# Another set of hand-set ranks for a scan-and-adapters kernel, with some gate steps and copies on other engines

## The chip, the core and the metric

The kernel runs on one core of a Trainium2 chip. The metric is the device time of one execution in microseconds (us); of several runs the median is given. A profiled execution has a time of its own and a span, which reaches from its first to its last instruction. A core has five engines that run side by side, each with its own queue of instructions, worked off in order: TensorE (PE in the profile; its weight loads are listed as PEld), VectorE (DVE), ScalarE (ACT), GpSimd (POOL) and SyncE (SP), which here only issues DMA transfers. PSUM is the memory that PE writes to, in eight banks; SBUF is the larger on-chip memory.

## The reference, cut to what matters

```python
def _attn_ref(a, b):              # a, b: (8, 6400, 128)
    for t in range(S):
        h = a[:, t] * h + b[:, t]
        out[:, t] = h
def _moe_ref(x, w_gate, A, B):    # x: out as (51200, 128); E = 8 adapters of rank 16
    logits = x @ w_gate
    topk = np.argpartition(-logits, 2, axis=1)[:, :2]
    w = exp(sel - max); w /= w.sum() + 1e-9
    delta[mask] += w[mask, k] * ((x[mask] @ A[e]) @ B[e])
    return x + delta
```

A linear recurrence along each of 8 sequences gives x. Then every one of the 51,200 rows goes through the two of eight small adapters whose logits are highest, weighted by a softmax over those two, and x is added. Read and written are 52.6 and 26.2 MB.

## The kernel before, in words

The rows are cut into 100 chunks of 512 rows (4 blocks of 128). A chunk goes through two halves.

The **front** of chunk c: a load of a and one of b bring two chunks (512 KB each) into one of 6 slots (line 709); PE transposes a into a bank of pA and b into a bank of pB (line 730; operations A, B and P); ScalarE copies pA to a_st (line 748, ae); VectorE runs the recurrence over 512 columns with one scan instruction (line 786, sc), which writes xT. Each scan needs the one before it.

Six blocks make a **unit**: PE multiplies xT with the adapters' A and the gate weights side by side (line 806, Z) and ScalarE copies the result to zl (line 812, ze). Four units make a **group** of 24 blocks; the first groups and the last ones are smaller, and the last four (18 to 21) hold a single chunk each. For a group the **gate** is worked out in small steps, named by kind and group, as 3_2 for kind 3 of group 2: kind 1, the largest logit (line 861, or 857 in groups of one chunk); 2, the difference to it (843 or 868); 3 and 5, the largest one masked out (845, 848); 4, the second largest (850); 6, the difference to that (852 or 870); 7, the sum of both (874); w1, a sigmoid on ScalarE (876); 8, the weights g (882). Kinds 1, 4 and 8 always run on VectorE. Kinds 2, 3, 5, 6 and 7 run on GpSimd, unless the list GATE_DVE names them.

The **back** of a chunk: zw = zl times g (line 915 on GpSimd, mu; line 919 on VectorE for the chunks in MU_DVE, md); PE transposes zw into a bank (928, T); a copy brings it to zwT (te: line 934 on ScalarE for the chunks in TE_ACT, else line 937 on VectorE); PE adds xT and zwT times B up in the same bank (942 and 943, D); a copy brings the result to outt (line 957 on ScalarE, oe; line 954 on VectorE for the chunks in OE_DVE, od); a store takes two chunks to the output, of the last four chunks one (line 988, st). outt holds 18 chunks. The banks of pO are used in turn for the back; for the last 12 chunks those of pA and pB are used too.

**What sets the order.** Nothing of this order is written in the program's text as such. Every operation has a rank, a base that grows with its chunk, plus an entry of TEMPLATE by its kind and its place in a period of six chunks, plus an entry of NUDGE by its name. `Program.schedule` (line 332) goes through a model of the engines with operations sorted by rank on each: an engine takes the one of lowest rank once its inputs are there by the model, and if no engine can go on, the operation that could start first of all. The result is one fixed list for each engine, and `waits` (line 402) puts in the semaphore waits. A rank is thus a wish; where an operation's inputs come later than its rank, others go ahead only when all engines are stuck. SyncE's list holds loads (la, lb) and stores (st) in one queue, and a load waits there until PE has read the slot's earlier content.

Of the kernel before, what the change touches and what calls it, by code (L numbers as in the profile page):

```python
# [30 lines left out]
    "A0": 332.698, "A1": 444.438, "A2": 395.795, "A3": 404.345, "A4": 42.259, "B0": 448.161, "B1": 453.245, "B2":  # L31
    404.853, "B3": 403.799, "B99": 126.44, "D0": 64.669, "D1": 46.767, "D10": 83.067, "D11": 50.451, "D12": 30.005,
    "D13": 96.239, "D14": 46.691, "D15": 42.568, "D16": 45.565, "D17": 47.157, "D18": 49.305, "D19": 50.496, "D2":
    38.555, "D20": 51.923, "D21": 47.721, "D22": 49.736, "D23": 51.873, "D24": 54.021, "D25": 55.177, "D26": 56.604,
    "D27": 52.402, "D28": 54.23, "D29": 56.021, "D3": 33.278, "D30": 58.169, "D31": 59.312, "D32": 60.739, "D33":
    56.537, "D34": 58.365, "D35": 60.156, "D36": 62.304, "D37": 63.447, "D38": 64.874, "D39": 60.672, "D4": 32.746,
    "D40": 62.5, "D41": 64.291, "D42": 67.109, "D43": 67.982, "D44": 69.439, "D45": 65.237, "D46": 67.065, "D47":
    68.968, "D48": 71.116, "D49": 72.307, "D5": 37.683, "D50": 73.734, "D51": 69.532, "D52": 71.36, "D53": 73.151,
    "D54": 75.554, "D55": 76.442, "D56": 77.884, "D57": 73.682, "D58": 75.51, "D59": 78.992, "D6": 33.975, "D60":
    80.547, "D61": 81.42, "D62": 82.877, "D63": 79.28, "D64": 79.738, "D65": 84.028, "D66": 84.486, "D67": 87.103,  # L40
    "D68": 88.306, "D69": 84.321, "D7": 39.991, "D70": 86.2, "D71": 87.403, "D72": 90.164, "D73": 91.555, "D74":
    93.991, "D75": 88.603, "D76": 92.856, "D77": 92.398, "D78": 96.983, "D79": 95.164, "D8": 78.702, "D80": 99.794,
    "D81": 93.491, "D82": 115.278, "D83": 119.134, "D84": 158.466, "D85": 222.925, "D86": 154.578, "D87": 119.577,
    "D88": 117.659, "D89": 187.618, "D9": 48.932, "D90": 118.7, "D91": 181.167, "D92": 131.702, "D93": 144.905,
    "D94": 212.656, "D95": 160.549, "D96": 168.236, "D97": 95.555, "D98": 78.117, "D99": 130.788, "P10": 15.657,
    "P11": 22.702, "P12": 39.886, "P13": 53.646, "P14": 28.955, "P15": 9.673, "P16": 15.966, "P17": 18.415, "P18":
    15.425, "P19": 16.467, "P20": 18.575, "P21": 20.345, "P22": 21.434, "P23": 23.734, "P24": 20.558, "P25": 21.527,
    "P26": 22.774, "P27": 25.117, "P28": 26.674, "P29": 27.984, "P30": 24.567, "P31": 25.76, "P32": 28.665, "P33":
    31.023, "P34": 32.839, "P35": 33.584, "P36": 30.178, "P37": 31.969, "P38": 33.403, "P39": 35.194, "P4": 49.375,
    "P40": 37.555, "P41": 38.3, "P42": 34.859, "P43": 36.65, "P44": 38.084, "P45": 39.912, "P46": 41.703, "P47":  # L50
    42.448, "P48": 38.994, "P49": 40.785, "P5": 25.498, "P50": 42.219, "P51": 44.047, "P52": 45.838, "P53": 46.583,
    "P54": 43.129, "P55": 44.92, "P56": 46.354, "P57": 48.182, "P58": 49.973, "P59": 51.388, "P6": 21.844, "P60":
    47.694, "P61": 49.485, "P62": 50.919, "P63": 52.747, "P64": 54.65, "P65": 55.395, "P66": 51.989, "P67": 53.78,
    "P68": 55.214, "P69": 57.042, "P7": 43.001, "P70": 58.833, "P71": 59.833, "P72": 56.139, "P73": 57.93, "P74":
    59.364, "P75": 61.192, "P76": 62.525, "P77": 64.45, "P78": 61.014, "P79": 62.469, "P8": 16.186, "P80": 65.142,
    "P81": 67.722, "P82": 69.826, "P83": 70.391, "P84": 67.243, "P85": 68.614, "P86": 69.735, "P87": 76.775, "P88":
    74.219, "P89": 78.609, "P9": 48.708, "P90": 71.884, "P91": 73.91, "P92": 151.293, "P93": 167.423, "P94": 136.89,
    "P95": 80.922, "P96": 88.01, "P97": 133.589, "P98": 99.826, "T0": 56.382, "T1": 91.427, "T10": 73.644, "T11":
    39.89, "T12": 41.046, "T13": 32.168, "T14": 85.598, "T15": 40.536, "T16": 43.441, "T17": 44.977, "T18": 47.615,
    "T19": 49.081, "T2": 99.35, "T20": 50.954, "T21": 46.745, "T22": 48.179, "T23": 49.148, "T24": 52.331, "T25":  # L60
    53.797, "T26": 55.635, "T27": 51.426, "T28": 52.86, "T29": 54.688, "T3": 26.004, "T30": 56.479, "T31": 57.945,
    "T32": 59.77, "T33": 55.561, "T34": 56.995, "T35": 58.823, "T36": 60.614, "T37": 62.08, "T38": 63.905, "T39":
    59.696, "T4": 30.392, "T40": 61.13, "T41": 62.958, "T42": 64.749, "T43": 66.885, "T44": 68.47, "T45": 64.261,
    "T46": 65.695, "T47": 67.523, "T48": 69.426, "T49": 70.892, "T5": 35.969, "T50": 72.765, "T51": 68.556, "T52":
    69.99, "T53": 71.818, "T54": 73.609, "T55": 75.33, "T56": 76.915, "T57": 72.706, "T58": 74.14, "T59": 75.968,
    "T6": 44.458, "T60": 77.301, "T61": 80.323, "T62": 81.908, "T63": 77.335, "T64": 78.671, "T65": 81.565, "T66":
    82.439, "T67": 85.689, "T68": 86.658, "T69": 82.764, "T7": 38.572, "T70": 84.097, "T71": 85.976, "T72": 87.861,
    "T73": 89.94, "T74": 92.377, "T75": 87.346, "T76": 89.832, "T77": 90.32, "T78": 95.622, "T79": 94.176, "T8":
    37.375, "T80": 98.697, "T81": 90.642, "T82": 104.934, "T83": 107.397, "T84": 147.188, "T85": 128.013, "T86":
    190.078, "T87": 133.961, "T88": 186.597, "T89": 94.992, "T9": 42.025, "T90": 132.176, "T91": 95.557, "T92":  # L70
    169.538, "T93": 158.037, "T94": 309.895, "T95": 232.152, "T96": 128.695, "T97": 143.342, "T98": 164.952, "T99":
    82.392, "Z0": -4.337, "Z1": 19.058, "Z10": 20.035, "Z11": 18.061, "Z12": 19.964, "Z13": 22.981, "Z14": 26.095,
    "Z15": 23.194, "Z16": 25.272, "Z17": 27.295, "Z18": 29.086, "Z19": 26.745, "Z2": 33.243, "Z20": 29.505, "Z21":
    33.201, "Z22": 34.768, "Z23": 32.132, "Z24": 34.381, "Z25": 37.372, "Z26": 39.509, "Z27": 36.813, "Z28": 39.062,
    "Z29": 41.866, "Z3": 20.134, "Z30": 43.657, "Z31": 40.948, "Z32": 43.197, "Z33": 46.001, "Z34": 47.792, "Z35":
    45.083, "Z36": 47.332, "Z37": 50.136, "Z38": 51.927, "Z39": 49.567, "Z4": 8.718, "Z40": 51.897, "Z41": 54.701,
    "Z42": 56.492, "Z43": 53.943, "Z44": 56.192, "Z45": 58.996, "Z46": 60.787, "Z47": 58.078, "Z48": 60.342, "Z49":
    63.146, "Z5": 29.08, "Z50": 64.937, "Z51": 63.005, "Z52": 65.559, "Z53": 69.201, "Z54": 71.664, "Z55": 70.67,
    "Z56": 72.956, "Z57": 75.978, "Z58": 78.531, "Z59": 74.133, "Z6": 18.876, "Z60": 75.768, "Z61": 79.931, "Z62":
    81.463, "Z63": 79.056, "Z64": 80.664, "Z65": 116.582, "Z66": 110.873, "Z67": 170.833, "Z68": 78.231, "Z7":  # L80
    52.026, "Z8": 23.141, "Z9": 12.774, "ae0": 377.319, "ae1": 447.239, "ae10": 20.203, "ae11": 45.845, "ae12":
    26.555, "ae13": 114.601, "ae14": 78.247, "ae15": -8.915, "ae16": 9.547, "ae17": 35.333, "ae18": 14.62, "ae19":
    16.327, "ae2": 430.204, "ae20": 17.024, "ae21": 19.433, "ae22": 21.246, "ae23": 22.239, "ae24": 18.539, "ae25":
    21.584, "ae26": 22.556, "ae27": 23.782, "ae28": 26.079, "ae29": 27.602, "ae3": 401.457, "ae30": 23.062, "ae31":
    25.957, "ae32": 28.958, "ae33": 29.47, "ae34": 31.955, "ae35": 33.668, "ae36": 29.441, "ae37": 31.155, "ae38":
    32.869, "ae39": 34.329, "ae4": 24.476, "ae40": 36.772, "ae41": 38.486, "ae42": 34.157, "ae43": 35.871, "ae44":
    37.584, "ae45": 38.889, "ae46": 40.717, "ae47": 42.508, "ae48": 38.305, "ae49": 40.019, "ae5": 44.251, "ae50":
    41.733, "ae51": 43.092, "ae52": 44.852, "ae53": 46.643, "ae54": 42.44, "ae55": 44.154, "ae56": 45.868, "ae57":
    47.159, "ae58": 48.987, "ae59": 50.778, "ae6": 13.042, "ae60": 47.245, "ae61": 48.959, "ae62": 50.673, "ae63":
    51.895, "ae64": 53.609, "ae65": 55.455, "ae66": 51.252, "ae67": 52.966, "ae68": 54.68, "ae69": 56.087, "ae7":  # L90
    61.054, "ae70": 57.847, "ae71": 59.638, "ae72": 55.69, "ae73": 57.404, "ae74": 59.117, "ae75": 60.339, "ae76":
    62.053, "ae77": 65.098, "ae78": 61.47, "ae79": 61.896, "ae8": 2.461, "ae80": 63.047, "ae81": 66.773, "ae82":
    69.416, "ae83": 71.087, "ae84": 65.544, "ae85": 67.471, "ae86": 72.468, "ae87": 71.251, "ae88": 123.456, "ae89":
    94.229, "ae9": 43.382, "ae90": 106.289, "ae91": 132.603, "ae92": 144.806, "ae93": 134.759, "ae94": 74.716,
    "ae95": 79.344, "ae96": 74.12, "ae97": 78.144, "ae98": 107.257, "ae99": 242.941, "cc": 482.303, "ch": 444.183,
    "cm": 407.091, "g1_0": -93.951, "g1_1": 24.384, "g1_10": 53.547, "g1_11": 58.272, "g1_12": 62.407, "g1_13":
    66.495, "g1_14": 73.075, "g1_15": 96.367, "g1_16": 144.379, "g1_17": 89.89, "g1_18": 186.375, "g1_19": 157.094,
# [1009 lines left out]
```

## Time and profile before

| what | value |
|---|---|
| median of 3 runs | 202.56 us (202.31 to 202.83) |
| profiled execution, its own time | 202.71 us |
| its span | 200.9 us |
| granted clock of TensorE, mean | 0.992 |
| moved by DMA | 79.26 MB |

How to read what follows: a row of a group has line, engine, operation, names and shapes, count, busy time and mean length of one. A row of a timeline has start, length, engine, line, operation, output and inputs, the count, and in brackets how long the engine had been idle and what ended it; rows of one kind that follow one another are merged. A row of a window has its limits and length, the busy time of the five engines' columns, the granted clock, the share of time that the 16 DMA engines were busy, and the GB/s. Tiles go by the program's names without buffer numbers.

### The profile page before, as it was taken

What the parts mean: (1) busy time and instruction counts of PE and PEld (TensorE: products, weight loads), DVE (VectorE), ACT (ScalarE), POOL (GpSimd) and SP (SyncE); (2) the same over time, 40 slices, a digit from 0 to 9 for tenths busy, and PEclk for the clock granted to TensorE, in tenths of its full rate; (3) what the DMA queues carried; (4) which work ended last, traced back from release to release, by engine and by line L of the source; (5) the groups of instructions that cost most, each with busy time, mean ns of one, the idle gap of its engine ahead of it and who ended that gap; (6) DMA issues with size and microseconds to landing.
All of it is one profiled execution on the core that took longest, in us unless ns stands there. A gap on an engine that the chain in (4) does not pass through costs nothing.

```text
span 200.9 us, 7616 instructions
## 1 busy us (share of the span) xinstructions
PE 179.4 (89%) x3192; PEld 156.7 (78%) x3192; DVE 175.8 (88%) x283; ACT 175.7 (87%) x327; POOL 136.6 (68%) x176
## 2 busy tenths in 40 slices
PE   6988888999899989996998999889999998998970
PEld 6876767888678878886887888778887887887850
DVE  1599899999999988998797999898899999999970
ACT  2479898999879989998897999899989998999870
POOL 1331549598999988697787797867956657867320
PEclk9999999999999999999999999999999999999996
DMA  6999999999999999999999999999999999999985
GB/s 211 399 410 405 407 409 402 409 409 404 420 400 402 393 415 404 408 413 411 408 412 409 410 409 416 413 409 410 412 410 409 417 411 408 402 385 385 373 339 203
DMA packets 29065, 79.26 MB, mean 395 GB/s; under 512 B 2664, under 2 KB 2920, under 8 KB 29032
## 3 DMA queue, kind: packets, MB, share of 16 engines
q1 hardware_dynamic: 28456, 78.39, 98.9%
q8 instruction: 25, 0.41, 0.8%
q10 hardware_dynamic: 576, 0.40, 0.6%
q14 instruction: 8, 0.07, 0.1%
HBM read 52.56 MB, written 26.21 MB: 392 GB/s over the span
## 4 chain that ended last, share of the span: by engine, by line
DMA 33%; PE 28%; ACT 8%; DVE 8%; issue 1%; SPq 1%; ACTq 0%
DMA a_tm<-in_a_dram 26%; DMA b_tm<-in_b_dram 7%; PE pO L942 5%; PE pZ L806 4%; PE pB L730 4%; PE pA L730 4%; DVE xT L786 4%; PE pO L928 4%; PE pO L943 4%; ACT zl L812 3%; ACT a_st L748 2%; ACT outt L957 2%; ACT zwT L934 1%; DVE zwT L937 1%; SPq L709 1%
## 5 line engine op out<-in xcount | busy, mean ns | idle before, releaser
L786 DVE TENSOR_TENSOR_SCAN xT<-a_st,xT,pB 128x512 f16<-128x512 f32 x96 | 120.5, 1255 | 6.5 <-PE pA L730 2.9
L915 POOL TENSOR_TENSOR zw<-zl,g 128x512 f16<-128x512 f32 x88 | 92.7, 1066 | 26.5 <-DVE g L882 19.3
L730 PE MATMUL pB<-ident_f,b_tm 64*128 64x64 f32 (+1 forms) x784 | 69.6, 230 | 6.1 <-DMA a_tm<-in_a_dram 5.6
L730 PE MATMUL pA<-ident_f,a_tm 64*128 64x64 f32 (+1 forms) x784 | 69.7, 230 | 0.6 <-DMA b_tm<-in_b_dram 0.3
L748 ACT COPY a_st<-pA 128x512 f32<-128x512 f32 x100 | 62.9, 634 | 4.9 <-PE pA L730 3.6
L730 PEld LDWEIGHTS pB<-ident_f,b_tm 64*128 64x128 f32 (+1 forms) x784 | 56.7, 139 | 11.1 <-DMA a_tm<-in_a_dram 7.3
L812 ACT COPY zl<-pZ 128x816 f32<-128x816 f32 (+1 forms) x69 | 59.6, 863 | 2.4 <-PE pZ L806 2.3
L730 PEld LDWEIGHTS pA<-ident_f,a_tm 64*128 64x128 f32 (+1 forms) x784 | 56.8, 139 | 6.1 <-DMA b_tm<-in_b_dram 0.7
L957 ACT COPY outt<-pO 128x512 f32<-128x512 f32 x87 | 55.0, 641 | 2.5 <-PE pO L943 2.2
L942 PE MATMUL pO<-ident_h,xT 128*128 128x128 f16 x368 | 51.4, 222 | 1.3 <-ACT zwT L934 1.1
L943 PE MATMUL pO<-cst_h,zwT 128*128 128x128 f16 x368 | 50.3, 219 | 0.0
L942 PEld LDWEIGHTS pO<-ident_h,xT 128*128 128x128 f16 x368 | 40.3, 113 | 4.4 <-ACT zwT L934 1.6
L806 PE MATMUL pZ<-cst_h,xT 128*128 128x136 f16 x400 | 36.0, 225 | 4.0 <-DVE xT L786 2.0
L943 PEld LDWEIGHTS pO<-cst_h,zwT 128*128 128x128 f16 x368 | 36.8, 100 | 0.0
L928 PE MATMUL pO<-ident_h,zw 128*128 128x128 f16 x368 | 35.2, 220 | 1.4 <-DVE outt L954 0.5
L806 PEld LDWEIGHTS pZ<-cst_h,xT 128*128 128x128 f16 x400 | 26.2, 115 | 8.6 <-DVE xT L786 4.2
L928 PEld LDWEIGHTS pO<-ident_h,zw 128*128 128x128 f16 x368 | 22.7, 97 | 4.9 <-issue 1.3
L937 DVE COPY zwT<-pO 128x512 f16<-128x512 f16 x57 | 23.0, 409 | 4.0 <-PE pO L928 3.6
L934 ACT COPY zwT<-pO 128x512 f16<-128x512 f16 x35 | 21.8, 627 | 4.4 <-PE pO L928 4.0
L852 POOL TENSOR_TENSOR L<-k,m 128x192 f32<-128x192 f32 (+2 forms) x16 | 8.3, 519 | 6.5 <-DVE m L850 6.5
L874 POOL TENSOR_TENSOR k<-k,L 128x192 f32<-128x192 f32 (+1 forms) x17 | 9.4, 554 | 4.5 <-DVE L L870 3.2
L848 POOL TENSOR_TENSOR L<-L,k 128x192 f32<-128x192 f32 (+1 forms) x15 | 8.6, 576 | 5.4 <-DVE L L845 4.7
(58 smaller groups left out, 113.3 us busy)
## 6 DMA issues: line engine op xcount, KB each, us to landing
a_tm<-in_a_dram SPq DMA_DIRECT2D x48, 512.0 KB, 13.1
b_tm<-in_b_dram SPq DMA_DIRECT2D x48, 512.0 KB, 13.2
out_dram<-outt SPq DMA_DIRECT2D x47, 512.0 KB, 13.1
a_tm<-in_a_dram SPq DMA_DIRECT2D x4, 256.0 KB, 4.2
out_dram<-outt SPq DMA_DIRECT2D x4, 256.0 KB, 4.0
b_tm<-in_b_dram SPq DMA_DIRECT2D x3, 256.0 KB, 5.7
out_dram<-outt SPq DMA_DIRECT2D x1, 496.0 KB
b_tm<-in_b_dram ACTq DMA_DIRECT2D x1, 256.0 KB, 3.4
```

Of the source, the lines that this page charges most:

```text
L730: last = eng["pe"].transpose(*args)
L748: lambda: eng["act"].copy(a_st[c % NA][:, :], pA[:, c % 2, :]), fr(c, "ae"))
L786: last = eng["dve"].tensor_tensor_scan(out=x[:, s0:s1], data0=a_st[c % NA][:, s0:s1], data1=pB[:, c % 2, s0:s1], initial=init, op0=ALU.mul ...
L806: last = eng["pe"].matmul(pZ[:, k // (n // 2), o : o + W], xblock(b0 + k), Awg_h)
L812: return eng["act"].copy(zl[:, zb : zb + n, :].rearrange("p (h k) w -> p h (k w)", h=2), pZ[:, :, 0 : n // 2 * W])
L915: lambda: eng["pool"].tensor_tensor(out=wv, in0=zv, in1=gv, op=ALU.mult), ba(gi, c, "mu"))
L928: last = eng["pe"].transpose(ptile[:, k * 128 : k * 128 + 128], zz[:, k, :], ident_h[:, :])
L934: lambda: eng["act"].copy(zt, ptile[:, 0 : n * 128]), ba(gi, c, "ta"))
L937: lambda: eng["dve"].tensor_copy(zt, ptile[:, 0 : n * 128]), ba(gi, c, "te"))
L942: eng["pe"].matmul(dst, xblock(b0 + k), ident_h[:, :], start=True, stop=False)
L943: last = eng["pe"].matmul(dst, zt[:, k * 128 : k * 128 + 128], B_h, start=False, stop=True)
L957: lambda: eng["act"].copy(ov, bv), ba(gi, c, "oe"))
```

## The change

The ranks come from another seed of the same search. The program's code is the same; only constants differ.

```diff
-GATE_DVE = ['2_0', '2_14', '2_18', '3_1', '3_11', '3_13', '3_15', '3_16', '3_2', '3_8', '5_14', '5_17', '6_0', '6_18', '6_3', '7_1', '7_17', '7_18', '7_20', '7_21']
+GATE_DVE = ['2_14', '2_18', '3_1', '3_11', '3_13', '3_15', '3_16', '3_8', '5_14', '5_17', '6_3', '7_17', '7_18', '7_2', '7_20', '7_21']
...
-TE_ACT = [0, 1, 2, 6, 7, 11, 12, 19, 22, 24, 25, 30, 31, 36, 37, 42, 43, 48, 49, 54, 55, 59, 60, 61, 67, 68, 69, 73, 75, 78, 80, 82, 83, 87, 92, 93, 95, 96, 97, 98]
+TE_ACT = [0, 1, 2, 6, 7, 11, 12, 19, 24, 25, 30, 31, 36, 37, 42, 43, 48, 49, 54, 55, 60, 61, 67, 68, 69, 73, 74, 75, 78, 80, 82, 83, 87, 90, 92, 93, 94, 95, 96, 97, 98]
 MU_DVE = [61, 72, 77, 82, 86, 91, 92, 93, 94, 96, 97, 99]
-OE_DVE = [11, 15, 72, 81, 92, 94, 97]
+OE_DVE = [11, 15, 72, 81, 86, 92, 94, 96, 97]
...
 TEMPLATE = {
-    "la": [0.617, 1.382, -0.181],
-    "lb": [0.289, -1.881, 0.376],
+    "la": [1.102, 2.627, 1.579],
+    "lb": [2.514, 4.938, 1.652],
...
-    "sc": [-0.352, 0.601, 0.068, 1.247, 29.666, -1.078],
+    "sc": [-0.772, -0.302, -0.229, 45.175, 60.592, -0.968],
...
-    "st": [2.655, 0.241, 1.338],
+    "st": [2.764, 1.849, -0.699],
```

The templates of the other kinds differ in the same way, most by less than 1 where the middle of the run uses them. Of NUDGE, some 480 of 1,288 entries differ, nearly all for chunks below 18 and from 78 on; the entries of the middle are the same, such as these:

```python
"lb56": 32.697, "la58": 33.962, "st24": 58.826, "st26": 61.432, "st28": 65.231
```

The list of gate steps on VectorE has 16 names and had 20 (2_0, 3_2, 6_0, 6_18 and 7_1 leave, 7_2 comes). ScalarE's list of zwT copies has 41 chunks and had 40 (22 and 59 leave, 74, 90 and 94 come). VectorE's list of output copies has 9 and had 7 (86 and 96 come). Number, shapes and contents of all operations and transfers are the same.

More of the change, by code (lines that the diff above doesn't have):

```diff
@@ L245 @@
 TEMPLATE = {
-    "la": [0.617, 1.382, -0.181],
-    "lb": [0.289, -1.881, 0.376],
-    "A": [0.0, 0.0, 0.0, 0.0, -22.609, 0.0],
-    "B": [0.016, -0.127, 0.808, 0.22, 0.59, 0.13],
-    "ae": [0.478, 0.108, 0.156, -0.214, 0.098, 0.802],
-    "sc": [-0.352, 0.601, 0.068, 1.247, 29.666, -1.078],
-    "Z": [0.074, 0.124, 0.07, -0.415],
-    "ze": [0.146, 0.091, -0.438, 0.663],
-    "g1": [0.736],
-    "g2": [-2.194],
-    "g3": [-0.858],
-    "g4": [-0.178],
-    "g5": [18.025],
-    "g6": [22.851],
-    "w1": [-0.215],
+    "la": [1.102, 2.627, 1.579],
+    "lb": [2.514, 4.938, 1.652],
+    "A": [0.0, 0.0, 0.0, 0.0, 8.835, 0.0],
+    "B": [0.009, -0.256, 0.344, -0.056, 1.151, 0.453],
+    "ae": [0.72, 0.104, -0.01, 0.181, 0.043, 0.887],
+    "sc": [-0.772, -0.302, -0.229, 45.175, 60.592, -0.968],
+    "Z": [-0.11, 0.237, -0.045, -0.342],
+    "ze": [0.744, -0.171, -0.004, 0.826],
+    "g1": [13.688],
+    "g2": [5.03],
+    "g3": [-2.196],
+    "g4": [-1.086],
+    "g5": [31.806],
+    "g6": [21.26],
+    "w1": [-0.301],
     "w2": [0.0],
@@ L264 @@
     "p3": [0.0],
-    "mu": [1.432, -0.247, 0.712, 0.979, 0.638, 1.684],
-    "T": [-0.04, 0.011, 0.309, 0.056, 0.263, 0.069],
-    "te": [-0.194, -0.349, -1.1, 4.512, 0.878, -1.627],
-    "D": [0.293, 0.3, -0.403, 0.26, 0.471, 0.206],
-    "oe": [-0.17, -1.066, 0.732, 0.378, -0.33, -0.315],
-    "st": [2.655, 0.241, 1.338],
-    "ta": [0.113, -0.235, -1.676, 1.106, 0.524, -0.261],
-    "md": [60.131, 24.961, 1.624, -2.633, 1.124, -17.851],
+    "mu": [-0.029, -0.944, -0.301, 0.352, 0.288, 1.547],
+    "T": [-0.048, -0.432, 0.073, 0.471, 0.308, 0.135],
+    "te": [-0.952, -0.199, -0.346, 14.078, -4.494, -2.03],
+    "D": [-0.056, 0.355, -0.103, 0.22, 0.375, 0.132],
+    "oe": [-0.295, -0.102, 0.821, 0.666, 0.029, -0.305],
+    "st": [2.764, 1.849, -0.699],
+    "ta": [30.336, -6.933, -5.212, 1.29, 0.829, 38.329],
+    "md": [43.885, 7.675, 42.269, -10.074, -0.09, -40.307],
     "wu": [0.0],
     "fi": [0.0, 0.0, 0.0, 0.0, 0.0, 0.0],
-    "ch": [53.69],
-    "cm": [11.639],
-    "cc": [8.728],
+    "ch": [92.955],
+    "cm": [20.146],
+    "cc": [40.014],
     "mb": [0.0],
-    "q2": [-0.491],
-    "q3": [-4.197],
-    "q5": [-3.568],
-    "q6": [0.447],
-    "q7": [0.367],
+    "q2": [0.997],
+    "q3": [-4.705],
+    "q5": [-3.63],
+    "q6": [-0.349],
+    "q7": [-0.116],
     "q8": [0.0],
-    "g7": [19.938],
-    "g8": [-0.285],
+    "g7": [-14.036],
+    "g8": [-0.055],
 }
```

350 rows, old and new, of the table NUDGE are left out of this document.

## The prediction

> **What bounds the kernel now.** I read first the page's top, for engine totals and the slices, and then the tables by window, from coarse to fine.
>
> ```profile
> span 200.9 us, 7616 instructions
> ## 1 busy us (share of the span) xinstructions
> PE 179.4 (89%) x3192; PEld 156.7 (78%) x3192; DVE 175.8 (88%) x283; ACT 175.7 (87%) x327; POOL 136.6 (68%) x176
> ...
> GB/s 211 399 410 405 407 409 402 409 409 404 420 400 402 393 415 404 408 413 411 408 412 409 410 409 416 413 409 410 412 410 409 417 411 408 402 385 385 373 339 203
> ...
> q1 hardware_dynamic: 28456, 78.39, 98.9%
> ```
>
> No engine is full over the whole span, but the DMA queue q1 is, at 98.9%. From the second slice to the 34th it moves about 410 GB/s. Only the last six slices (5.02 us each) fall away. The reader is to see two regimes: a long middle in which the transfers set the pace whatever the engines do, and a tail of some 30 us in which they don't.
>
> ```profile
> 140.00:160.00 20.00, 18.94 (x358) 16.63 (x357) 18.67 (x29) 19.22 (x37) 13.99 (x17) 1.00 1.03 410
> 160.00:170.00 10.00, 9.25 (x169) 7.84 (x167) 9.59 (x15) 9.03 (x18) 6.20 (x9) 1.00 1.04 413
> 170.00:175.00 5.00, 4.67 (x93) 4.09 (x91) 5.00 (x9) 5.00 (x10) 4.18 (x6) 1.00 1.01 401
> ...
> 180.00:185.00 5.00, 4.36 (x66) 3.68 (x65) 5.00 (x21) 4.92 (x11) 3.89 (x5) 1.00 1.04 395
> ```
>
> The columns are PE, PEld, VectorE, ScalarE and GpSimd busy, then the granted clock, the DMA share and GB/s. In the middle VectorE still has 1.3 us free in 20 (18.67). From 170 us it has none, and at 180 to 185 ScalarE has almost none. So in the tail VectorE is the engine to watch. In the finer windows:
>
> ```profile
> 185.00:186.00 1.00, 1.00 (x21) 0.95 (x19) 0.60 (x3) 0.67 (x2) 1.00 (x4) 1.00 0.89 340
> ...
> 188.00:189.00 1.00, 0.89 (x10) 0.51 (x10) 1.00 (x7) 1.00 (x4) 0.00 (x0) 1.00 0.87 334
> ...
> 191.00:192.00 1.00, 0.36 (x7) 0.18 (x4) 1.00 (x3) 0.83 (x2) 0.95 (x1) 1.00 0.90 336
> 192.00:193.00 1.00, 0.93 (x12) 0.69 (x12) 0.97 (x5) 0.94 (x3) 0.00 (x0) 1.00 0.52 195
> ```
>
> The DMA engines go hungry there: 0.11 + 0.13 + 0.10 + 0.48 = 0.82 us of idle transfer time in these four microseconds. Who keeps them hungry is seen in VectorE's own timeline:
>
> ```profile
> 189.36 0.41 DVE L937 COPY zwT<-pO 128x512 f16<-128x512 f16 x1
> 189.74 0.22 DVE L874 TENSOR_TENSOR k<-k,L 128x32 f32<-128x32 f32 x1
> 189.88 0.78 DVE L919 TENSOR_TENSOR zw<-zl,g 128x512 f16<-128x512 f32 x1
> 190.62 0.19 DVE L882 SCALAR_TENSOR_TENSOR g<-L,sd 128x32 f32<-128x32 f32 x1
> 190.73 0.68 DVE L954 COPY outt<-pB 128x512 f32<-128x512 f32 x1
> 191.33 0.68 DVE L954 COPY outt<-pO 128x512 f32<-128x512 f32 x1
> 191.93 0.18 DVE L874 TENSOR_TENSOR k<-k,L 128x32 f32<-128x32 f32 x1
> 192.03 0.68 DVE L919 TENSOR_TENSOR zw<-zl,g 128x512 f16<-128x512 f32 x1
> ```
>
> The gate step at 191.93 stands behind two output copies, and the zw product at 192.03, from which one of the last four chunks is made, stands behind it. Instructions overlap a little, so what one costs is the distance from start to start: 0.60 us for an output copy (190.73 to 191.33), 0.38 for a zwT copy (189.36 to 189.74), 0.10 for a small gate step (191.93 to 192.03).
>
> **The change part by part.** The profiled execution took 202.71 us, 200.9 of them span and 1.81 around it. It lies 0.15 above the median of 202.56. I make the sum as a difference and put it on the median.
>
> Whether a name stands in a list decides its engine. Off VectorE go the gate steps 2_0, 3_2, 6_0, 6_18 and 7_1; 7_2 comes to it. The zwT copies of chunks 74, 90 and 94 go to ScalarE, those of 22 and 59 to VectorE. The output copies of chunks 86 and 96 go to VectorE. Most of this lies where transfers set the pace. The dearest piece is 3_2:
>
> ```profile
> L845 POOL TENSOR_SCALAR L<-k x10: 539/858/863, 36.1 to 177.6; 128x192 f32<-128x192 f32 x9, 128x96 f32<-128x96 f32 x1
> L845 DVE TENSOR_SCALAR L<-k x7: 168/233/260, 15.7 to 172.4; 128x192 f32<-128x192 f32 x6, 128x64 f32<-128x64 f32 x1
> ```
>
> ```profile
> 189.87 0.24 POOL L870 TENSOR_TENSOR L<-zl,v 128x32 f32<-128x32 f32 x1
> ```
>
> It grows from 0.233 to 0.858 us on the way to group 2's gates, in the first 30 us. That makes those products 0.63 us later. The loads don't wait for it, and they hide it. Were that cover gone, it would cost 0.63. The other early gate steps (2_0, 6_0, 7_1, 7_2) are smaller; 7_1 on 64 elements on GpSimd is not in the trace, and I bound it by the 0.24 of the last row (32 elements) and 0.86 (192), and take 0.24, the shape nearest in size. 7_2, 192 elements, I bound on VectorE by 0.10 and 0.60, the smallest and largest step above, and take 0.23, the 192-element step of line 845. These too, and chunks 22, 59 and 74 in the middle, I cost at nothing: the cover is the full DMA queue (410 GB/s at 140 to 160 us). Without it, chunks 22 and 59 would cost VectorE 2 x 0.38.
>
> What counts is the tail, with chunks 86, 90, 94 and 96 and step 6_18. Rows for the same kinds:
>
> ```profile
> 185.57 0.42 DVE L937 COPY zwT<-pO 128x512 f16<-128x512 f16 x1 [0.40 <-PE pO L928]
> 185.91 0.41 DVE L937 COPY zwT<-pA 128x512 f16<-128x512 f16 x1
> ```
> ```profile
> 188.85 1.12 ACT L934 COPY zwT<-pB 128x512 f16<-128x512 f16 x2
> 189.87 0.60 ACT L957 COPY outt<-pO 128x512 f32<-128x512 f32 x1
> 190.34 0.24 ACT L876 ACTIVATE sd<-k 128x32 f32<-128x32 f32 x1
> ```
>
> - The output copies of 86 and 96: VectorE +2 x 0.60 = +1.20 us. ScalarE loses two steps of about 0.48 (189.87 to 190.34) and wins two zwT copies of about 0.5 (two of them fill 188.85 to 189.87). So its tail load stays even, and I take nothing for it.
> - The zwT copy of 94, at most the one at 189.36: VectorE -0.34 to -0.38; I take 0.34, since it must now queue on ScalarE, which is busy without a gap there. What queues behind it is the output copy at 189.87.
> - The zwT copy of 90 lies near 185 us, where VectorE waits 0.40 us for PE (first row above). What goes there only lengthens that wait: between 0 and 0.34, I take 0.
> - Step 6_18: 0.10 off VectorE.
>
> Sum: +1.20 - 0.34 - 0.10 = **+0.76 us** on an engine that has no idle time from 170 to 192.5 but for the gaps at 185 to 187 us. That is 203.47 beside the profiled run, and 203.32 on the median. Its bounds: 0 if both output copies fall into gaps, 1.20 if nothing that leaves was on the path.
>
> GpSimd's share of 6_18 beside a VectorE product can be read at 189.88: 0.78 us for the product there, while GpSimd ran its step of 189.87, and 0.68 for the one at 192.03, alone. So such company costs 0.10. The Trainium skill, SBUF — State Buffer, section "SBUF: two separate sides", says more: a GpSimd instruction and a VectorE one with two SBUF inputs shut each other out for the whole instruction. By that rule 6_18 on GpSimd (0.24 us) would be paid in full by the product beside it and the sum would be near 1.00, so 203.6 us; the 0.10 of this trace does not bear it out.
>
> **The ranks** are the part that the profile prices worst. About 480 of the nudges differ, all at the two ends, and the templates differ for all chunks. SyncE's queue can be read off them in the middle:
>
> ```profile
> 83.58 0.49 SPq L709 DMA_DIRECT2D b_tm<-in_b_dram  x1
> 84.12 2.93 SPq L988 DMA_DIRECT2D out_dram<-outt  x2
> 87.09 1.32 SPq L709 DMA_DIRECT2D a_tm<-in_a_dram  x1
> 88.46 1.04 SPq L988 DMA_DIRECT2D out_dram<-outt  x1
> ```
>
> ```profile
> b_tm<-in_b_dram SPq DMA_DIRECT2D x48, 512.0 KB, 13.2
> ```
>
> By base + template + nudge, lb56 has 54 - 1.881 + 32.697 = 84.8, st24 85.5, st26 85.7, la58 87.8, st28 90.6: b, two stores, a, a store, as the rows show. After, lb56 has 54 + 4.938 + 32.697 = 91.6, behind st24, st26, st28 (88.5) and la58 (89.5): four transfers of 512 KB, at 410 GB/s 1.28 us each, so 5.1 us later, and once in each period of six chunks. I cost it at nothing, because the queue moves as many bytes in whatever order and a transfer lands 13 us after its issue (the last column of the b_tm row), so the loads ahead still feed PE. If that cover goes, PE stalls on b_tm instead of a_tm, up to one transfer (1.28) at the end. At the ends too many operations are held back until something else frees them for me to read an order from the ranks. There the bounds are the rivals.
>
> **Rivals.**
> (1) *Faster.* The new order puts the gate steps of the last groups ahead of the output copies. The step at 191.93 had its inputs at 190.11, when the GpSimd step of 189.87 shown above ended; it waited 1.8 us in VectorE's queue, 1.20 of it behind two output copies. Passing them would start the last products 1.20 earlier. What the end can win is limited by the hungry DMA time, 0.82 us: 202.56 - 0.82 = 201.7; with the 0.34 of the zwT copy on top, 201.4. It decides as soon as the two copies come after the last gate step. For it speaks that the DMA share falls to 0.52 just behind those copies; against it, that the change adds copies of that very kind.
> (2) *No change that can be measured.* The two added copies fall into VectorE's gaps (0.40 at 185.57 is one) or wait for PE anyway, and the order is as good as the old one: 202.6, or up to +0.4.
> (3) *Slower through the loads.* lb56 and its likes come too late and one transfer is missed at the end: 202.56 + 1.28 = 203.8. For it: the chain of waits in the middle runs through such loads,
>
> ```profile
> 93.66 12.68 DMA a_tm<-in_a_dram
> ```
>
> so PE does use them as they land. Against it: the full DMA share all the while.
>
> **How the numbers follow.** A measurement of this kernel can tell about 0.3% (0.6 us) from no change. The forecast (+0.76, VectorE's tail) has 0.36, the faster rival 0.32, no change 0.25, the load rival 0.07. So slower by over 0.3% 0.43, within 0.25, faster 0.32. The time is that of the forecast, 203.3 us; alone it reaches from 202.6 to 203.8. As both signs hold much, the range reaches from the faster rival with the zwT copy (201.4) to the forecast with one missed transfer (203.32 + 1.28 = 204.6).
>
> **What would show it.** Right: VectorE's tail full for longer than to 192.5 us, with more output copies of line 954 in its timeline than before (its two at 190.73 and 191.33 are shown above), one of them ahead of a late zw product, and the span's last slices with fewer GB/s. The gate step of line 845 at 0.86 us once more on GpSimd, without trace in the end. SyncE's order with b_tm behind three stores, and 400 to 415 GB/s all the same. Wrong: a DMA share near 1 through 192 to 193 us, or PE idle for b_tm in the middle with the GB/s falling below 400. What I can't read is the order at the two ends; if the result misses, most likely by that.

## The result and the profile after

The changed kernel took 203.28 us in the median (202.34 to 203.71, 20 runs), the kernel before 202.57 us (202.23 to 203.61, 20 runs) beside it. The ratio is 1.0028 with a 95% interval of 1.0016 to 1.0039, so the change costs 0.57 us (0.32 to 0.79). The two medians lie 0.71 apart; the text goes by the ratio throughout and gives the medians where they say something else. The profiled execution took 203.55 us.

The page of the changed kernel, whole span: busy time of the engines, GB/s in 40 slices, and the queue that carries loads and stores.

```profile
span 201.6 us, 7623 instructions
...
PE 179.1 (89%) x3192; PEld 156.2 (77%) x3192; DVE 177.0 (88%) x280; ACT 175.7 (87%) x326; POOL 138.8 (69%) x180
...
GB/s 208 372 416 409 409 406 410 402 407 412 411 399 410 417 408 410 406 413 405 416 404 415 404 410 413 411 411 409 415 411 410 411 413 410 387 390 383 369 331 178
...
q1 hardware_dynamic: 28456, 78.39, 98.6%
```

The reader sees the same two regimes. The second slice is poorer than before (372 against 399 GB/s), and the middle runs at 399 to 417, about as before. VectorE and GpSimd carry 1.2 and 2.2 us more. The next two rows are windows of the end (columns as in the prediction), and under them stands VectorE's timeline there.

```profile
185.00:186.00 1.00, 1.00 (x20) 0.97 (x19) 0.87 (x4) 0.29 (x2) 1.00 (x4) 1.00 0.99 383
...
192.00:193.00 1.00, 0.67 (x12) 0.67 (x12) 1.00 (x4) 0.84 (x3) 0.28 (x1) 1.00 0.52 191
```
```profile
185.52 0.69 DVE L954 COPY outt<-pO 128x512 f32<-128x512 f32 x1
```
```profile
189.97 0.22 DVE L874 TENSOR_TENSOR k<-k,L 128x32 f32<-128x32 f32 x1 [0.29 <-POOL L L870]
190.12 0.78 DVE L919 TENSOR_TENSOR zw<-zl,g 128x512 f16<-128x512 f32 x1
...
191.06 0.68 DVE L954 COPY outt<-pB 128x512 f32<-128x512 f32 x1
191.66 0.68 DVE L954 COPY outt<-pO 128x512 f32<-128x512 f32 x1
192.26 0.18 DVE L874 TENSOR_TENSOR k<-k,L 128x32 f32<-128x32 f32 x1
...
193.18 0.69 DVE L919 TENSOR_TENSOR zw<-zl,g 128x512 f16<-128x512 f32 x1
...
195.96 0.69 DVE L954 COPY outt<-pA 128x512 f32<-128x512 f32 x1 [0.58 <-PE pA L943]
```

The two added output copies are at 185.52 (chunk 86) and 195.96 (chunk 96). The first stands where VectorE used to wait for PE. The second is VectorE's last instruction, behind the last product. Where the zwT copy of 94 was, VectorE now idles 0.29 us for GpSimd (189.97). Still, the last product starts at 193.18 us instead of 192.85, which is 0.33 later.

In these two traces most of that 0.33 is there before any of the tail's copies. VectorE's timeline around the scans of chunks 91 to 93, after first, then before (counted through VectorE's list, the scan at 169.43 us is that of chunk 93; the expectations below call it the scan of chunk 95):

```profile
165.88 1.28 DVE L786 TENSOR_TENSOR_SCAN xT<-a_st,xT,pB 128x512 f16<-128x512 f32 x1 [0.39 <-PE pA L730]
...
167.99 1.27 DVE L786 TENSOR_TENSOR_SCAN xT<-a_st,xT,pB 128x512 f16<-128x512 f32 x1
169.36 0.36 DVE L882 SCALAR_TENSOR_TENSOR g<-L,sd 128x192 f32<-128x192 f32 x1
169.64 1.27 DVE L786 TENSOR_TENSOR_SCAN xT<-a_st,xT,pB 128x512 f16<-128x512 f32 x1
```
```profile
165.51 1.27 DVE L786 TENSOR_TENSOR_SCAN xT<-a_st,xT,pB 128x512 f16<-128x512 f32 x1
...
167.99 1.27 DVE L786 TENSOR_TENSOR_SCAN xT<-a_st,xT,pB 128x512 f16<-128x512 f32 x1
169.18 0.33 DVE L882 SCALAR_TENSOR_TENSOR g<-L,sd 128x192 f32<-128x192 f32 x1
169.43 1.27 DVE L786 TENSOR_TENSOR_SCAN xT<-a_st,xT,pB 128x512 f16<-128x512 f32 x1
```

Scan 91 (first row of each) waits 0.39 us for PE and starts 0.37 later. Scan 92 starts at 167.99 in both. Scan 93 starts 0.21 later, behind a gate step (L882) that starts 0.18 later, and what follows it is 0.20 to 0.49 later. From scan 93 to the last product it is 23.42 us before and 23.54 after. So these traces put 0.21 us ahead of scan 93 and 0.12 on the tail itself. Why PE is late at 165 us stands in PE's timeline and in the chain of waits of after:

```profile
165.13 0.27 PE L730 MATMUL pB<-ident_f,b_tm 64*128 64x64 f32 x1 [0.68 <-DMA a_tm<-in_a_dram]
```
```profile
152.05 13.04 DMA a_tm<-in_a_dram
...
165.13 0.27 PE pB L730
...
165.88 1.28 DVE xT L786
```

PE is idle 0.68 us for a load of a. It is that of chunks 92 and 93 (PE transposes the b of chunk 91 and the a of chunk 92 in turn, as one operation): the new list of SyncE issues la94 ahead of la92 and lb92, the old one issued la92, a store and lb92 first. Before, PE starts this operation earlier and without a wait, and waits for a load of b at the next one:

```profile
164.49 0.27 PE L730 MATMUL pB<-ident_f,b_tm 64*128 64x64 f32 x1
...
166.57 0.27 PE L730 MATMUL pA<-ident_f,a_tm 64*128 64x64 f32 x1 [0.34 <-DMA b_tm<-in_b_dram]
```

Since scan 92 starts at the same time in both, the lateness does not reach scan 93 through the scans. It can through the gate: a GpSimd product that waits for PE, two gate steps behind it and ScalarE's sigmoid come later too (after first, then before):

```profile
166.72 1.07 POOL L915 TENSOR_TENSOR zw<-zl,g 128x512 f16<-128x512 f32 x1 [0.77 <-PE pO L928]
168.97 0.36 ACT L876 ACTIVATE sd<-k 128x192 f32<-128x192 f32 x1
```
```profile
166.31 1.06 POOL L915 TENSOR_TENSOR zw<-zl,g 128x512 f16<-128x512 f32 x1
168.74 0.37 ACT L876 ACTIVATE sd<-k 128x192 f32<-128x192 f32 x1
```

### The profile page after: what moved, and what is told of

Its sections match the earlier page's. It is cut to its first block, busy times and chain, and to the rows that moved or that the text cites. A ratio compares the mean times of both kernels' runs of the same rounds, so it can differ in the third digit from the quotient of the medians.

```text
span 201.6 us, 7623 instructions
## 1 busy us (share of the span) xinstructions
PE 179.1 (89%) x3192; PEld 156.2 (77%) x3192; DVE 177.0 (88%) x280; ACT 175.7 (87%) x326; POOL 138.8 (69%) x180
## 4 chain that ended last, share of the span: by engine, by line
PE 30%; DMA 27%; ACT 11%; DVE 9%; POOL 4%; issue 3%; SPq 0%
DMA a_tm<-in_a_dram 21%; DMA b_tm<-in_b_dram 6%; DVE xT L786 6%; PE pA L730 5%; PE pZ L806 5%; PE pO L942 5%; PE pO L928 5%; PE pB L730 4%; PE pO L943 4%; ACT outt L957 3%; ACT a_st L748 3%; POOL zw L915 3%; ACT zl L812 2%; ACT zwT L934 2%; DVE zwT L937 1%
## 5 line engine op out<-in xcount | busy, mean ns | idle before, releaser
L730 PE MATMUL pB<-ident_f,b_tm 64*128 64x64 f32 (+1 forms) x784 | 68.8, 230 | 4.0 <-DMA a_tm<-in_a_dram 3.3
L730 PE MATMUL pA<-ident_f,a_tm 64*128 64x64 f32 (+1 forms) x784 | 68.9, 230 | 3.4 <-DMA b_tm<-in_b_dram 2.9
L730 PEld LDWEIGHTS pA<-ident_f,a_tm 64*128 64x128 f32 (+1 forms) x784 | 56.2, 139 | 9.1 <-DMA b_tm<-in_b_dram 4.2
L934 ACT COPY zwT<-pO 128x512 f16<-128x512 f16 x35 | 21.2, 615 | 1.4 <-PE pO L928 1.2
L786 DVE TENSOR_TENSOR_SCAN xT<-a_st,pB 128x512 f16<-128x512 f32 (+1 forms) x8 | 7.5, 940 | 5.9 <-PE pB L730 5.7
```

The lines of the kernel that those rows point to most:

```text
L730: last = eng["pe"].transpose(*args)
L786: last = eng["dve"].tensor_tensor_scan(out=x[:, s0:s1], data0=a_st[c % NA][:, s0:s1], data1=pB[:, c % 2, s0:s1], initial=init, op0=ALU.mul ...
L934: lambda: eng["act"].copy(zt, ptile[:, 0 : n * 128]), ba(gi, c, "ta"))
```

## The experiments

Twelve kernels, each timed beside the kernel before on the same chip, all with the lists of every engine fixed, so that an edit moves nothing but what its diff shows. Each had 12 runs, `h_after_then_before` 8. "Before" took 202.54 to 202.71 us in them. The table gathers them with the marks of their traces in us: start of scan 93, start of the last product (chunk 99), end of the last output copy, and the span.

| kernel | ratio [95%] | scan 93 | last product | last copy ends | span |
|---|---|---|---|---|---|
| before | 1 | 169.43 | 192.85 | 196.26 | 200.9 |
| after | 1.0028 [1.0016, 1.0039] | 169.64 | 193.18 | 196.65 | 201.6 |
| a_loads_before | 1.0011 [0.9992, 1.0029] | 169.51 | 193.06 | 196.54 | 200.8 |
| a_out_on_act | 1.0020 [1.0002, 1.0038] | 169.69 | 193.12 | 196.53 | 200.7 |
| a_te94_dve | 1.0042 [1.0026, 1.0058] | 169.66 | 193.07 | 196.55 | 201.2 |
| b_out_on_dve | 1.0010 [0.9996, 1.0025] | 169.83 | 193.36 | 196.84 | 200.8 |
| b_loads_after | 1.0006 [0.9992, 1.002] | 169.46 | 192.88 | 196.29 | 200.3 |
| b_te94_act | 1.0023 [1.0, 1.0045] | 169.60 | 193.28 | 196.69 | 200.8 |
| b_od85_full | 1.0003 [0.9982, 1.0023] | 169.40 | 194.15 | 197.56 | 201.6 |
| b_od94_late | 0.9983 [0.9966, 1.0] | 169.44 | 192.76 | 196.23 | 200.7 |
| h_before_then_after | 1.0021 [1.0011, 1.0031] | 169.09 | 192.65 | 196.13 | 200.5 |
| h_after_then_before | 1.0033 [1.0017, 1.005] | 169.78 | 193.20 | 196.61 | 201.3 |
| b_st96_act | 1.0014 [0.9994, 1.0034] | 169.44 | 192.88 | 196.29 | 200.6 |
| b_new_tail | 1.0009 [0.9989, 1.0029] | 168.93 | 191.78 | 194.96 | 200.5 |

Most executions lie within 1 us of the median, a few farther (201.92 to 204.30 in one series of before). So a trace shows what happened in one execution, and only the ratio says what an edit is worth. Scan 93 starts between 168.93 and 169.83 in kernels with the same lists up to it, so 0.21 between two traces is no finding by itself. 0.001 is 0.2 us.

### Parts of the change undone or done alone

**a_loads_before**: the changed kernel with SyncE's whole list of before, of which this is the place that the traces point at.

```diff
-sp: ... st56 lb90 la94 la92 lb92 st58 lb94 ...
+sp: ... st56 lb90 la92 st58 lb92 la94 lb94 ...
```

> The kernel after with SyncE's list of before (loads and stores), all other lists as after. Theory of the forecast (the output copies of 86 and 96 on VectorE make the tail longer): no effect, ratio to before stays near 1.003. Theory of the loads (la94 ahead of la92 makes chunk 92's transposes late, and 0.2 us of that stays to the end): about 0.2 us comes back, ratio near 1.002, and the scan that starts at 169.64 us in the trace of after starts near 169.4.

202.80 us, 1.0011: by the ratios some 0.34 of the 0.57 us are gone, but the intervals of the two overlap, so this is not shown. The chain of waits has no load in it any more around 165 us. It runs through ScalarE instead:

```profile
164.87 0.49 ACT a_st L808
165.37 0.50 ACT outt L1017
165.91 1.27 DVE xT L846
```

(Lines are 60 higher in this kernel.) The wait for the load is gone, and scan 91 starts at 165.91 all the same: other work was nearly as late.

**b_loads_after**: the same list the other way round, in the kernel before.

> The kernel before with SyncE's list of after (loads and stores in the order of after), every other engine's list as before. Theory of the loads: a part of the loss comes with the order of the last loads (la94 ahead of la92, after which the scan of chunk 95 started at 169.64 us instead of 169.43 and all that hangs on it came 0.21 later): 202.55 + 0.2 to 0.4, so 202.75 to 202.95, ratio about 1.0015. The forecast's theory (VectorE's two output copies) and the theory that the landing of loads scatters by chance from kernel to kernel: no change, 202.55, ratio 1.000.

202.68 us, 1.0006 [0.9992, 1.002]. PE waits for the load here too (0.64 us at 164.96), yet the time hardly moves (from 0.16 less to 0.41 us more by the interval). It may be that the order of the loads costs something only in company with the new lists of the other engines. These two runs fit that, but do not show it.

**a_out_on_act** and **b_out_on_dve**: the output copies of 86 and 96 put back on ScalarE in after (shown), and moved to VectorE in before, at after's places.

```diff
-dve: ... te91 od86 ... te99 od97 od96
+dve: ... te91 ... te99 od97
-act: ... oe87 ... oe99
+act: ... oe87 oe86 ... oe99 oe96
```

> The kernel after with the output copies of chunks 86 and 96 back on ScalarE. Theory of the forecast: 0.76 us come back (two copies of 0.60 less what left VectorE anyway), ratio to before near 0.999. Rival (the two copies fall into VectorE's gaps at 185 us and behind its last work): no change, ratio near 1.003, and VectorE idle near 185.5 us in their place.

> The kernel before with only the output copies of chunks 86 and 96 put on VectorE, at the places they have after. Theory of the forecast: +0.8 to +1.2 us, ratio 1.004 to 1.006. Rival (they fall into gaps): at most +0.2 us, ratio 1.000 to 1.001.

1.0020 against 1.0028 for undoing, 1.0010 for doing: 0.16 and 0.20 us for both copies together, where the forecast had 1.20. The intervals leave room for some 0.5 us, not for 1.20 (doing it alone costs at most 0.51).

**a_te94_dve** and **b_te94_act**: the zwT copy of 94, back on VectorE in after, onto ScalarE in before (shown; the output copy of 95 goes behind the sigmoid w1_20, as it stands in after).

```diff
-dve: ... g1_20 g1_21 te94 g7_20 md97 ...
+dve: ... g1_20 g1_21 g7_20 md97 ...
-act: ... te93 oe95 w1_20 ...
+act: ... te93 te94 w1_20 oe95 ...
```

> The kernel after with the zwT copy of chunk 94 back on VectorE, between the largest logits of group 21 and the gate step 7 of group 20, as before. Theory of the forecast: VectorE has 0.34 us more in its tail, ratio 1.004 to 1.005. Rival (on ScalarE it stands ahead of group 20's sigmoid and makes that 0.1 to 0.3 us late, while VectorE idles 0.29 us at 189.7): 0.1 us comes back, ratio 1.002, and the weights of group 20 come near 190.85 instead of 190.95 us.

> The kernel before with the zwT copy of chunk 94 on ScalarE, right behind that of 93, the sigmoid w1_20 behind it. The forecast counted 0.34 us off VectorE's tail for this: 202.2, ratio 0.998. The reading of the trace of after (VectorE idle 0.29 us where the copy was, and w1_20 0.28 us later, which holds up g8_20): 202.55 to 202.65, ratio 1.000 to 1.0005. The run of the reverse edit in after (203.20 against 203.28 of after) agrees with the second.

Undone, 1.0042 [1.0026, 1.0058] instead of 1.0028, where the forecast's theory had it. Done alone, 1.0023 [1.0, 1.0045], with medians only 0.19 us apart. The two point in opposite directions, and neither is clear of no effect, so the times leave this copy open. In the trace of `b_te94_act` the copy's time on VectorE is not won:

```profile
189.92 0.22 DVE L874 TENSOR_TENSOR k<-k,L 128x32 f32<-128x32 f32 x1 [0.29 <-POOL L L870]
...
193.05 0.19 DVE L882 SCALAR_TENSOR_TENSOR g<-L,sd 128x32 f32<-128x32 f32 x1 [0.16 <-ACT sd L876]
193.28 0.69 DVE L919 TENSOR_TENSOR zw<-zl,g 128x512 f16<-128x512 f32 x1
```

VectorE waits 0.29 us for GpSimd's small steps, which the copy used to cover, and 0.16 for ScalarE, which is now the later one. The trace of the undoing agrees: its last product starts 23.41 us after scan 93, and 23.54 in after.

### Two halves

**h_before_then_after** and **h_after_then_before**: all engines follow the lists of one kernel up to about 169.4 us and those of the other from there, copies and gate steps on the engines of the list in force. From scan 92 to scan 97 the lists of PE, VectorE, ScalarE and GpSimd are the same in both kernels, so the exact place of the change matters little.

> Every engine's list of before up to the scan of chunk 95 (about 169.4 us), and from there the lists of after, with its engines for the copies and gate steps (output copies of 86 and 96 on VectorE, zwT copies of 90 and 94 on ScalarE, 6_18 on GpSimd). If the loss arises in the tail, as the forecast has it: 202.57 + 0.57, about 203.1, ratio 1.0028. If it arises before the scan of chunk 95 (loads, head, early gate steps): 202.6, ratio 1.000. If neither place has it alone: between, 1.001 to 1.002.

> The other half: every engine's list of after up to the scan of chunk 95, from there the lists and engines of before. If the loss arises in the tail: 202.6, ratio 1.000. If it arises before the scan of chunk 95: about 203.1, ratio 1.0028 (in the trace of after that scan started 0.21 us later, which alone would be 1.001). The two halves should add up to 1.0028 if nothing else plays a part.

1.0021 for the new tail alone, 1.0033 for the new front alone, 1.0028 for both. Neither place has the loss alone: 0.43 us (0.22 to 0.63) for the tail and 0.67 (0.34 to 1.01) for the front, against 0.57 for both. The sum of the halves is larger than the whole, but with intervals this wide that is hardly a contradiction. The front alone, with the tail of before, costs as much as the whole change.

The other runs agree about the front. Four kernels follow all lists of after up to scan 93 (after, `a_out_on_act`, `a_te94_dve`, `h_after_then_before`): ratios of 1.0020 to 1.0042, medians 0.46 to 0.71 us above that of before beside them. The nine others have ratios of 0.9983 to 1.0023, which overlap with these a little, and medians from 0.24 below to 0.26 above, which don't. Among the nine are `a_loads_before`, with after's lists but for SyncE's, and `b_loads_after`, with SyncE's alone. In the traces scan 93 starts at 169.64 to 169.78 in the four, and at 168.93 to 169.83, mean 169.40, in the eight with all lists of before up to there. That is a difference in the mean, not in each trace.

What in the front costs the time is not separated further. Besides the loads at 165 us there is the head: from 5 to 10 us the five kernels with after's lists on the four other engines move 345 to 375 GB/s, the nine with those of before 376 to 399. The means lie 19 GB/s apart, which over 5 us is 0.1 MB, or by estimate 0.2 us at 410 GB/s, and a queue that stays full has no room to win it back before the tail. `a_loads_before` has the poor head too (373), so the head by itself doesn't make the loss. No run moved the head alone.

### What a copy costs in VectorE's full row

**b_od85_full**: the kernel before, and one output copy more on VectorE where it has no gap.

```diff
-act: ... oe85 oe84 ...
+act: ... oe84 ...
-dve: ... sc99 g1_18 ...
+dve: ... sc99 od85 g1_18 ...
```

> The kernel before with the output copy of chunk 85 on VectorE instead of ScalarE, right behind the scan of chunk 99, where VectorE has no gap. If a copy of 0.60 us costs its length wherever VectorE's row is full (the forecast's rule, its place alone chosen otherwise): 202.55 + 0.60 = 203.15, ratio 1.003. If the gaps behind it (0.40 us for PE at 185.57, and the time in which the last products wait for PE) take it up: 202.55 to 202.75, ratio 1.000 to 1.001.

1.0003 [0.9982, 1.0023]: not 0.60 us (at most 0.47). Yet the row did move: the last product starts 1.30 us later. The 0.60 became 1.30 by this (VectorE first, then GpSimd):

```profile
184.36 1.05 DVE L874 TENSOR_TENSOR k<-k,L 128x32 f32<-128x32 f32 x1
185.34 0.25 DVE L882 SCALAR_TENSOR_TENSOR g<-L,sd 128x96 f32<-128x96 f32 x1
```
```profile
184.26 1.11 POOL L915 TENSOR_TENSOR zw<-zl,g 128x512 f16<-128x512 f32 x1 [1.31 <-PE pO L928]
```

The small step that took 0.18 us in before now falls beside a product on GpSimd and takes 1.05. It ends 0.04 us after that product (185.37). The traced execution is the longest of this kernel's twelve (203.40 us against a median of 202.83), so its span of 201.6 overstates the edit.

**b_od94_late**: the kernel before, the output copy of 94 moved behind the last product.

```diff
-dve: ... g8_20 od92 od94 g7_21 md96 g8_21 md99 te99 od97
+dve: ... g8_20 od92 g7_21 md96 g8_21 md99 od94 te99 od97
```

> The kernel before with VectorE's output copy of chunk 94 moved from ahead of the gate step 7_21 to behind the last product (chunk 99). The forecast's rule and its rival (1) price this at 0.60 us earlier for the last products: 202.55 - 0.60 = 201.95, ratio 0.997. Theory that the end hangs on the last stores: SyncE issues the last four one after another, about 1 us each, from the moment that the output copy of chunk 98 is there; then earlier products are worth at most what they bring forward that copy, and the store of 92 and 94 goes out 1.3 us later and shares the end with the last four: 202.4 to 202.9, ratio 0.999 to 1.002.

0.9983 [0.9966, 1.0], between the two forecasts; the time alone, up to 0.69 us shorter, doesn't exclude the 0.60. The trace speaks against it: the last product starts at 192.76 instead of 192.85, 0.09 us for a copy of 0.60. VectorE, then GpSimd:

```profile
190.75 0.68 DVE L954 COPY outt<-pB 128x512 f32<-128x512 f32 x1
191.35 0.67 DVE L874 TENSOR_TENSOR k<-k,L 128x32 f32<-128x32 f32 x1
191.94 0.68 DVE L919 TENSOR_TENSOR zw<-zl,g 128x512 f16<-128x512 f32 x1
```
```profile
190.91 1.06 POOL L915 TENSOR_TENSOR zw<-zl,g 128x512 f16<-128x512 f32 x1 [0.77 <-DVE g L882]
```

The step 7_21 stands still until GpSimd's product ends at 191.97. The copy of 190.75 went on beside that product at its usual 0.68. So the place where od94 stood was one in which VectorE could not have done the gate step anyway.

The Trainium skill, SBUF — State Buffer, section "SBUF: two separate sides", states this as an exclusive lock: of a GpSimd instruction that reads SBUF and a VectorE one with two SBUF inputs the first to start holds the shared port pair for its whole length. The two rows of 0.67 and 1.05 us agree.

The prediction read the 0.78 us product at 189.88 as evidence against the rule. It is none. The held steps end 0.04 and 0.05 us after GpSimd's product, where such a step takes 0.18 alone, so about 0.13 of a VectorE instruction goes by while it is held. The product beside the GpSimd step that ended at 190.11 should then end at 190.11 + 0.68 - 0.13 = 190.66 (an estimate from these rows). It did: 189.88 + 0.78. So the 0.10 that it took longer is what a hold of 0.23 us leaves, not a sign that the two ran side by side.

### The end

**b_st96_act**: the kernel before, its last store issued by ScalarE.

```diff
-sp: ... st98 st97 st99 st96
+sp: ... st98 st97 st99
-act: ... oe99 oe96
+act: ... oe99 oe96 st96
```

> The kernel before with the store of chunk 96, the last one, issued by ScalarE right behind the output copy of 96 instead of by SyncE behind three other stores. In the trace of before SyncE started that issue at 197.10 us, 0.84 after the copy was done (196.26), and the transfers had three pauses of 0.2 to 0.4 us between the last four stores. Theory that SyncE's issues one after another set the end: 0.3 to 0.8 us earlier, 202.25 to 201.75, ratio 0.9985 to 0.996. Theory that the end is set by the bytes of the last stores and by the landing: 202.55, ratio 1.000.

The issue went out 0.78 us earlier (before, then this kernel):

```profile
195.94 1.12 SPq L988 DMA_DIRECT2D out_dram<-outt  x1
...
197.10 0.98 SPq L988 DMA_DIRECT2D out_dram<-outt  x1
```
```profile
196.32 0.36 ACTq L988 DMA_DIRECT2D out_dram<-outt  x1
```

The time did not follow: 202.78 us, 1.0014 [0.9994, 1.0034]. The theory that SyncE's one-after-another issues alone set the end, which had 0.9985 or less, falls. The Trainium skill, DMA: Bandwidth & Descriptors, section "Issuing engines are not separate DMA queues", says that issuing from several engines saves only the sequencer's time. This run agrees.

**b_new_tail**: the last 5 us put in an order that heeds what was found.

```diff
-pool: ... q6_21 mu98
+pool: ... q6_21
-dve: ... g8_20 od92 od94 g7_21 md96 g8_21 md99 te99 od97
+dve: ... g8_20 g7_21 md98 md96 g8_21 md99 od94 te99 od97
-act: ... oe95 w1_20 oe93 te97 w1_21 te98 oe98 te96 oe99 oe96
+act: ... oe95 w1_20 oe92 w1_21 oe93 te97 te98 te96 oe98 oe96 oe99
-pe: ... T97 T98 D97 D98 T99 T96 D99 D96
+pe: ... T97 T98 T96 D97 T99 D98 D96 D99
-sp: ... st98 st97 st99 st96
+sp: ... st98 st97 st96 st99
```

> The kernel before with another order of its last 5 us. GpSimd's last product (chunk 98, 190.89 to 191.95 in the trace of before) goes to VectorE, the output copy of 92 to ScalarE's idle time of 190.58 to 191.17; the gate step 7_21 goes ahead of the product of 98, the output copy of 94 behind that of 99, the output copy of 97 behind the zwT copy of 99; chunk 96 comes ahead of 98 and 99. In the run with the copy of 94 late the step 7_21 took 0.67 us (191.35 to 192.02) beside GpSimd's product, 0.18 in before; theory that the two shut each other out: without that product 7_21 takes 0.18 again, the product of 99 starts at about 192.2 instead of 192.85 and the last output copy ends at about 195.4 instead of 196.26: 202.56 less 0.5 to 0.9, 201.65 to 202.05, ratio 0.9955 to 0.9975. Theory that the end hangs on the pauses between the last stores alone: 202.3 to 202.8, ratio 0.999 to 1.001. If the forecast's rule held (copies and products cost their length on VectorE, whatever GpSimd does): one product of 0.60 us in, one copy of 0.60 out, no change for the product of 99 but for the order.

```profile
190.23 0.18 DVE L874 TENSOR_TENSOR k<-k,L 128x32 f32<-128x32 f32 x1
190.35 1.29 DVE L919 TENSOR_TENSOR zw<-zl,g 128x512 f16<-128x512 f32 x2
...
191.78 0.69 DVE L919 TENSOR_TENSOR zw<-zl,g 128x512 f16<-128x512 f32 x1
```

The step 7_21 takes 0.18 us without a GpSimd product beside it. Counted from scan 93, the last product starts 22.85 us later (23.42 in before) and the last copy ends 26.03 us later (26.83). And the time is that of before: 202.84 us, 1.0009 [0.9989, 1.0029]. The traced execution is the shortest of this kernel's twelve (202.49). Where the 0.80 us went is seen in the windows of the end:

```profile
196.00:197.00 1.00, 0.00 (x0) 0.00 (x0) 0.00 (x0) 0.00 (x0) 0.00 (x0) 1.00 0.77 299
197.00:198.00 1.00, 0.00 (x0) 0.00 (x0) 0.00 (x0) 0.00 (x0) 0.00 (x0) 1.00 0.68 260
```

All computing is over at 195 us, and the DMA engines still run with pauses (shares of 0.77 and 0.68) until 199. The last copy ends 4.6 us ahead of the span's end in before, 4.0 in `b_od85_full` and 5.5 here. By these three traces the stores take up what the engines win or lose. What spaces them is not shown. No version beats before beyond doubt: the best, `b_od94_late`, lies 0.17% below it with an interval that ends at 1.0.

## Why the prediction was right, and by which steps it was not

The time came where the forecast had it, slower by 0.28% where it said 0.38%. That lies on the border of the 0.3% that it called measurable, with an interval on both sides of it (0.16 to 0.39%). The way there was not the one it gave, so that the number fits is in good part luck.

- **Where the loss arises.** The forecast put all of it into the tail (+0.76). The tail alone costs 0.43 us (0.22 to 0.63). The front, priced at nothing but for a rival, costs 0.67 (0.34 to 1.01) with the tail of before.
- **What bounds the kernel.** The queue, as said. But that "in the tail VectorE is the engine to watch" failed: 1.30 us more on its row cost at most 0.47 us (`b_od85_full`), and 0.57 less won nothing (`b_new_tail`).
- **The output copies, 2 x 0.60 = 1.20.** This is the step that failed, and by the most: both together measure 0.16 to 0.20 us, with intervals that take in zero and not 1.20. The bound "0 if both fall into gaps" was the near one: 86 does, and 96 is the last instruction, behind the last product.
- **The rule "a copy costs its distance from start to start".** It holds only while the next instruction can use the time. Beside a GpSimd product a gate step can't (0.67 and 1.05 us instead of 0.18), so in the trace moving od94 won 0.09.
- **The zwT copy of 94, -0.34.** Open by the times: undone it costs 0.28 us more, done alone 0.47 more (from 0 to 0.91), and the two don't fit together. In the traces it was not won: GpSimd and ScalarE were the next late ones, at 0.29 and 0.16 us.
- **Step 6_18, -0.10.** No kernel moved it alone, so it stays open. The 0.10 by which its company lengthened a product was read rightly as a cost, but not as evidence against a lock.
- **The loads, costed at nothing.** In the middle the queue stayed at 399 to 417 GB/s. At the end la94 ahead of la92 makes PE wait 0.68 us. With the old list the ratio falls from 1.0028 to 1.0011, within overlapping intervals, so what the wait is worth is not shown. It is rival (3)'s place with half a transfer instead of a whole one, at a chance of 0.07.
- **Rival (1).** Its 1.20 us behind two copies were not to be had, since 7_21 was held by GpSimd for part of it and the end did not follow the last products.

So a term too large by a microsecond stood in for a loss that arises in good part elsewhere. What stays open: which part of the front costs the time (the loads at 165 us, the head, or both in company), what a single edit below 0.2% is worth, and what spaces the last stores.

The listed signs: more copies of line 954 in the tail, yes; one ahead of a late product, yes at 185.52, without its cost; fewer GB/s in the last slices, 331 and 178 against 339 and 203; b_tm behind three stores in the middle, yes, with 399 to 417 GB/s. VectorE's tail is full to 193 us, but with a new gap of 0.29 at 189.7. The page's row for line 845 on GpSimd shows the step once more, as said:

```profile
L845 POOL TENSOR_SCALAR L<-k x11: 539/858/864, 24.2 to 177.8; 128x192 f32<-128x192 f32 x10, 128x96 f32<-128x96 f32 x1
```

## What to carry to other kernels

An engine that is busy without a gap is not yet the bound: move one instruction on it, and see whether the end follows. Before a moved instruction is priced by its length, ask whether what stands behind it could have run in that time, or is held by another engine's work. Test a place by halves as well as by parts: here the parts of the tail, taken one by one, would not have shown that the front alone costs as much as the whole change. And a wait that is seen in one trace (0.68 us for a load) is a lead, not a cost, until undoing it moves the time beyond the noise.

## What was not expected of the hardware

- A small VectorE step of two SBUF inputs (128 x 32) takes 0.18 us alone and 0.67 or 1.05 beside a GpSimd product of 1.06 or 1.11 us. It ends 0.04 to 0.05 us after that product. A VectorE copy out of PSUM beside such a product kept its 0.68 us (`b_od94_late`, 190.75).
- SyncE's issues of the last 256 KB stores in before take 1.12 and 0.98 us (rows at `b_st96_act`) while the DMA engines pause. In `b_od94_late`, where a store of 512 KB goes out just ahead of the last four, there is no pause behind it. Windows of before, then of that kernel:

```profile
197.00:198.00 1.00, 0.00 (x0) 0.00 (x0) 0.00 (x0) 0.00 (x0) 0.00 (x0) 0.85 0.64 248
198.00:199.00 1.00, 0.00 (x0) 0.00 (x0) 0.00 (x0) 0.00 (x0) 0.00 (x0) 0.50 0.71 274
```
```profile
197.00:198.00 1.00, 0.00 (x0) 0.00 (x0) 0.00 (x0) 0.00 (x0) 0.00 (x0) 1.00 1.03 387
198.00:199.00 1.00, 0.00 (x0) 0.00 (x0) 0.00 (x0) 0.00 (x0) 0.00 (x0) 1.00 1.00 387
```

  Both spans end within 0.2 us of each other, since the latter has its pause ahead of these stores: a DMA share of 0.36 from 194 to 195 us, where before has 1.01.
